# Gates of four chunks computed as one batch on 128 partitions, in an mLSTM and feed-forward kernel

## The chip, the cores and the metric

One core of one Trainium2 chip. The metric is the device time of one launch in microseconds (us), which is the time of that core.

## The reference

Four sequences in a batch of 8 heads, 768 steps, head size 40, go through a recurrent mLSTM layer, and its output through a feed-forward layer:

```python
for t in range(S):
    m_new = np.maximum(f_gate[:, :, t] + m, i_gate[:, :, t])
    f_stab = np.exp(f_gate[:, :, t] + m - m_new); i_stab = np.exp(i_gate[:, :, t] - m_new); m = m_new
    C = f_stab * C + i_stab * v_t k_t^T          # one 40 x 40 state per sequence and head
    n = f_stab * n + i_stab * k_t
    y[:, :, t] = sigmoid(o_gate) * (C q_t) / max(|n q_t|, 1)
h = x @ w_in                                      # 3072 x 320 by 320 x 2048; x is y
g = h where h >= 1, 0 where h <= -1, (h + 1)^2 / 4 between
out = g @ w_out                                   # 2048 x 320
```

The two weights arrive as 8-byte floats and are turned into 4-byte ones on the chip.

## The kernel before

**Chunks and units.** The 768 steps are cut into six chunks of L = 128 steps, c = 0 to 5. Within a chunk the recurrence is written as matrix products. A unit n = 4c + b is chunk c of batch entry b, with its eight heads. For a unit: `score` (q k products on TensorE, 16 records `psa<-raw`), `decay` (eight exponentials on ScalarE into `Abc`), the product with the values (`psa<-v,Abc`, here called PV), the part from the state (`psa<-C,qn`), the normalizer `z`, the factor `sz` and the output `y` on VectorE, three transposes of `y` on TensorE (`psa<-ident,y`), and `xh`, `xl`, the high and low part of the transposed output. `carry_on` (L549) adds the unit to the state `C` (records `psa<-ow` or `psa<-v,vk`); between chunks GpSimd multiplies the state by `dec`.

**Gates.** For each chunk, `gate_sums` (L195), `gate_tail` (L241) and `gate_exps` (L255) work on 32 partitions, one for each pair of batch entry and head, 128 steps along the row. VectorE scans the running maximum `m` from the last chunk's `carry`; sums and differences give the log decays `a`; their coarse part `ah` and their rest are scanned into `ac` and `al`; four rows of 32 are collected in `ex`, transposed by one matmul, and exponentiated into `G`. `ac` is stored to memory (`a_d`) and loaded back spread over 128 partitions as `Abc`; the decay of the state goes through `dx`, `dc_d` and three loads of 4-byte elements into `dec` (`decays`, L293). Chunk 0 is done at the start (on 96 partitions, three copies of the 32). Chunk 1 is the `g1` at the end of STEPS, its tail after the first block of the loop. Chunks 2 to 5 are given out one step at a time from the loop steps 2, 13, 28 and 43 (GATES_AT, L51).

**The front.** STEPS (L57) is a written order of all engines' work up to the four units of chunk 0: `s` scores, `x` decays, `m` score products, `u` PV, `y`, `z`, `t` the rest of a unit, `E`, `A` exponents, `L` loads, `c`, `e`, `d` the conversion of the first weight slice, `wN` N matmuls on zeros ahead of the next ones.

**The loop.** Six token tiles of 512 (j) by 16 slices of 128 hidden columns (fc) make 96 steps x. `mm1` (L683), here block x, is eight matmuls into one of two PSUM buffers `psh`; ScalarE takes a ReLU and a square, VectorE the last step `r`, which frees the buffer. `mm2`, here product x, comes two steps later and adds to four PSUM buffers `pso`: eight records for j = 0, 24 after that. `slot` puts the pieces of the mLSTM units of the next token tile between the blocks.

**The weights.** Sixteen slices, in 0 to in 7 and out 0 to out 7, are loaded (`wraw`, two buffers) and converted by ScalarE (`mg`, and `wh` for the in slices), GpSimd and VectorE (`win`, `ow`, `mg`, `wl`). Block 2i and 2i + 1 need in i, products 2i and 2i + 1 need out i. A slice's load waits until the slice two before it is read.

**What sets the order.** Each engine runs its queue in order. Within STEPS the written order holds; after it, a scheduler places the instructions of each engine. All loads and stores are issued by SyncE (SP) to one queue. Tiles of the `gate` pool lie where those of the pool `mo` (`r`, `gh`, `gl`) come to lie after it is closed:

```python
    front = False
    gates.close()
    mo = ctx.enter_context(tc.tile_pool(name="mo", bufs=2))
```

Of the kernel before, what the change touches and what calls it, by code (L numbers as in the profile page):

```python
# [98 lines left out]
def mlstm_ffn_kernel(ctx, tc, qk, qn, vk, og, fi0, fi, w_in, w_out, cst, out):  # L99
# [95 lines left out]
    def gate_sums(c):  # L195
        pool, i, f = gsrc.pop(c)

        NP = NSEQ if c else 3 * NSEQ
        new = lambda name, p=NP, n=L, bufs=1: pool.tile([p, n], F32, name=name if c else name + "0", bufs=bufs)
        k = 1  # L200
        m, a, ah, ac = new("m", n=L + 1, bufs=k), f, new("ah", bufs=k), new("ac")
        al = ah

        ex = exs[c] = new("ex", P)
# [699 lines left out]
```

## Time and profile before

| | us |
|---|---|
| three timed runs | 519.98, 520.55, 523.67 |
| their median | 520.55 |
| span of the profiled execution, first to last instruction | 521.0 |

The profile is one execution taken by the hardware profiler. It gives no other time of its own than the span. Engines are PE (TensorE matmuls), PEld (its weight loads), DVE (VectorE), ACT (ScalarE), POOL (GpSimd) and SP (SyncE). Busy time is the time in which an instruction of the engine runs. Line numbers in rows of the trace are mostly those of the recording helper (L82 and L85), so that rows are told apart by the names of their tiles.

### The profile page before, as it was taken

How to read it: one execution, taken by the hardware profiler on the slowest of the kernel's cores; microseconds unless marked ns; L12 is line 12 of the kernel's file. 1: busy time of each engine (PE TensorE's matmuls, PEld its weight loads, DVE VectorE, ACT ScalarE, POOL GpSimd, SP SyncE). 2: the span in 40 equal slices, each digit the busy share in tenths (PEclk: the TensorE clock that was granted, in tenths of full speed). 3: DMA queues.
4: the chain of work that ended last, by engine and by line, in shares of the span. 5: the costliest groups of instructions: out<-in, count | busy, mean ns of one | idle time of the engine just before them, and what ended most of it. 6: DMA issues, size and time to landing. Idle time of an engine off the chain costs nothing. (4 is left out here: it accounts for less than half of the span.)

```text
span 521.0 us, 8909 instructions
## 1 busy us (share of the span) xinstructions
PE 493.2 (95%) x3396; PEld 419.9 (81%) x3399; DVE 355.5 (68%) x669; ACT 291.5 (56%) x576; POOL 144.3 (28%) x140
## 2 busy tenths in 40 slices
PE   8984999899898999989999989999999999999996
PEld 4753777678677889968898978889897889988986
DVE  4689987589669697777666778857656755534342
ACT  4626785345187745567643758554477544456553
POOL 2336624243334062242241344413220210000000
PEclk8987999979899999999999999999999999999999
DMA  7848555464441122343121254213432000010001
GB/s 234 274 138 295 155 155 172 110 211 133 131 144 42 26 81 87 89 129 96 45 87 41 82 173 127 72 62 95 146 102 77 15 1 2 0 52 1 1 1 51
DMA packets 29647, 51.30 MB, mean 98 GB/s; under 512 B 10124, under 2 KB 20004, under 8 KB 29604
## 3 DMA queue, kind: packets, MB, share of 16 engines
q1 hardware_dynamic: 29604, 50.72, 31.6%
q8 instruction: 27, 0.44, 0.4%
q14 instruction: 16, 0.13, 0.1%
HBM read 46.67 MB, written 4.04 MB: 97 GB/s over the span
## 5 line engine op out<-in xcount | busy, mean ns | idle before, releaser
L82 ACT ACTIVATE r<-psh,half 128x512 f32<-128x512 f32 x96 | 65.2, 684 | 102.8 <-PE psh L82 100.6
L82 PE MATMUL psh<-xh,wh 128*128 128x512 f32 x288 | 104.5, 419 | 10.1 <-DVE r L82 9.0
L82 DVE SCALAR_TENSOR_TENSOR r<-psh,r 128x512 f32<-128x512 f32 x96 | 65.9, 686 | 70.7 <-ACT r L82 69.8
L82 PE MATMUL pso<-oh,gh 128*128 128x320 f32 x320 | 99.2, 313 | 1.1 <-ACT gh L82 1.1
L82 PE MATMUL psh<-xh,wl 128*128 128x512 f32 x288 | 100.1, 401 | 0.0
L82 PE MATMUL pso<-ow,gh 128*128 128x320 f32 x320 | 98.6, 310 | 0.0
L82 PE MATMUL pso<-oh,gl 128*128 128x320 f32 x320 | 93.4, 313 | 0.2 <-DVE gl L82 0.2
L82 DVE TENSOR_TENSOR gl<-r,gh 128x512 fp32r<-128x512 f32 x80 | 62.3, 779 | 34.1 <-ACT gh L82 33.6
L82 ACT CAST gh<-r 128x512 fp32r<-128x512 f32 x80 | 49.4, 618 | 54.7 <-DVE r L82 52.3
L82 PEld LDWEIGHTS psh<-xh,wh 128*128 128x128 f32 x288 | 51.2, 193 | 20.0 <-DVE r L82 10.9
L82 PEld LDWEIGHTS psh<-xh,wl 128*128 128x128 f32 x288 | 55.0, 192 | 13.3 <-DVE m L85 0.4
L82 PEld LDWEIGHTS pso<-oh,gh 128*128 128x128 f32 x320 | 60.1, 188 | 5.1 <-ACT gh L82 1.7
L82 PEld LDWEIGHTS pso<-ow,gh 128*128 128x128 f32 x320 | 60.1, 188 | 2.8
L82 ACT ACTIVATE r<-r 128x512 f32<-128x512 f32 x96 | 60.4, 631 | 2.4
L82 PE MATMUL psh<-xl,wh 128*128 128x512 f32 x192 | 61.2, 400 | 0.0
L82 PEld LDWEIGHTS pso<-oh,gl 128*128 128x128 f32 x320 | 58.3, 188 | 1.5 <-DVE gl L82 0.8
L82 ACT ACTIVATE Abc<-Abc,nA 128x128 f32<-128x128 f32 x160 | 49.9, 393 | 1.5 <-POOL Abc L82 1.5
L82 POOL TENSOR_TENSOR v<-vk,G 128x328 f32<-128x328 f32 x36 | 32.0, 894 | 60.1 <-issue 33.6
L82 PEld LDWEIGHTS psh<-xl,wh 128*128 128x128 f32 x192 | 36.7, 191 | 8.2
L82 PE MATMUL pso<-ow,r 128*128 128x320 f32 x128 | 39.7, 454 | 1.0 <-DVE ow L82 1.0
L82 POOL TENSOR_SCALAR_AFFINE_SELECT Abc<-Abc 128x1024 f32<-128x1024 f32 x20 | 26.7, 1339 | 44.9 <-DMA Abc<-a_d 29.2
L82 POOL TENSOR_TENSOR C<-C,dec 120x369 f32<-120x369 f32 x16 | 14.0, 875 | 87.4 <-PE psa L82 87.4
(187 smaller groups left out, 719.6 us busy)
## 6 DMA issues: line engine op xcount, KB each, us to landing
Abc<-a_d SPq DMA_DIRECT2D x20, 512.0 KB
raw<-in_qk SPq DMA_DIRECT2D x48, 160.0 KB
vk<-in_vk SPq DMA_DIRECT2D x20, 324.0 KB
wraw<-in_w_in SPq DMA_DIRECT2D x8, 768.0 KB
wraw<-in_w_out SPq DMA_DIRECT2D x8, 640.0 KB
sig<-in_og SPq DMA_DIRECT2D x6, 640.0 KB
out<-r SPq DMA_DIRECT2D x24, 160.0 KB
qn<-in_qn SPq DMA_DIRECT2D x20, 180.0 KB
```

The costliest lines, as they stand in the source:

```text
L82: r = getattr(self.engine, name)(*args, **kwargs)
```

## The change

Chunks 1 to 4 get their gates at once, on 128 partitions (32 for each chunk), in the front and right behind it. Each partition scans its own history: a new input `fic` holds for chunk c the gates of chunks 1 to c, padded ahead with values that leave the running maximum as it is, 512 steps in all; the start is chunk 0's last maximum, which is now computed on all 128 partitions. The five steps are B0 to B4 in STEPS: B0 the scan on VectorE in the middle of the front, B1 and B3 on GpSimd, B2 on VectorE, B4 the four transposes, exponentials and the loads of `dec` for all four chunks. Tiles of the batch lie in the `gate` pool. Chunk 5 keeps the old way, from loop step 34. The diff's other edits rename the pieces of a unit in STEPS (`r`, `f`, `y`, `t`, `z` for `y`, `z`, `t`), split the work on `z`, `sz` and `y` at more places, and give `z` four buffers and `sz` two.

```diff
-GATES_AT = (2, 13, 28, 43)
+GATES_AT = 34
+NB = 4
...
-    "Lg Li Lo Lq0 Lv0 Lq1 Lw0 Lf Lq2 Lv2 Lq3 Lw1 Lc o w9 E0 g0 p A0 k0 x00 w2 s0 x01 m00 w1 E1 A1 h0 v0 x10 m01 w2 s1 "
-    "x11 v1 m10 c w2 u0 m11 w2 E2 A2 x20 w2 s2 y0 x21 v2 m20 m21 w2 u1 z0 w2 E3 A3 x30 e w2 s3 v3 y1 x31 t0 m30 m31 "
-    "w2 u2 z1 y2 w2 u3 t1 z2 y3 w2 t2 z3 t3 d g1 "
+    "Lg Li Lo Lq0 Lv0 Lq1 Lw0 Lq2 Lf Lv2 Lq3 Lw1 Lc o w9 E0 g0 q0 p A0 k0 x00 w2 s0 x01 m00 w1 E1 A1 h0 v0 x10 m01 w2 s1 "
+    "x11 v1 m10 c w2 u0 m11 w2 E2 A2 x20 B0 w2 s2 r0 f0 y0 x21 v2 m20 m21 w2 u1 t0 w2 E3 A3 x30 e w2 s3 v3 r1 f1 y1 x31 z0 "
+    "m30 m31 w2 u2 t1 r2 f2 y2 w2 u3 z1 t2 r3 f3 y3 w2 z2 t3 z3 d B1 B2 B3 B4 "
...
+    def batch_loads():
+        s = batch["s"] = gate.tile([P, 2, NB * L], F32, name="fi_s")
+        nc.sync.dma_start(s, fic)
+    def batch_maxima():
+        s = batch["s"]
+        m = gate.tile([P, NB * L + 1], F32, name="m_s")
+        nc.vector.tensor_copy(m[:, 0:1], batch["first"])
+        nc.vector.tensor_tensor_scan(out=m[:, 1:], data0=s[:, 0, :], data1=s[:, 1, :], initial=m[:, 0:1],
+                                     op0=ALU.add, op1=ALU.max)
+        batch["m"] = m[:, (NB - 1) * L:]
+    def batch_decays():
...
+        nc.gpsimd.tensor_tensor(out=a, in0=f, in1=m[:, :L], op=ALU.add)
+        nc.gpsimd.tensor_tensor(out=a, in0=a, in1=m[:, 1:], op=ALU.subtract)
+        nc.gpsimd.tensor_scalar(out=ah, in0=a, scalar1=CLAMP, scalar2=GRID, op0=ALU.max, op1=ALU.add)
+        nc.gpsimd.tensor_scalar(out=ah, in0=ah, scalar1=-GRID, scalar2=None, op0=ALU.add)
+        nc.gpsimd.tensor_copy(carry, m[(NB - 1) * NSEQ:, L:])
+    def batch_sums():
...
+        nc.vector.tensor_tensor_scan(out=ac, data0=rst, data1=ah, initial=0.0, op0=ALU.mult, op1=ALU.add)
+        nc.sync.dma_start(a_d[1:NB + 1].rearrange("c s l -> (c s) l"), ac)
+        nc.vector.scalar_tensor_tensor(out=a, in0=a, scalar=CLAMP, in1=ah, op0=ALU.max, op1=ALU.subtract)
...
+        nc.vector.tensor_tensor_scan(out=al, data0=rst, data1=a, initial=0.0, op0=ALU.mult, op1=ALU.add)
+    def batch_tail():
...
+        eng = nc.gpsimd
+        eng.tensor_tensor(out=a, in0=i, in1=m[:, 1:], op=ALU.subtract)
+        eng.tensor_tensor(out=a, in0=a, in1=al, op=ALU.subtract)
+        eng.tensor_tensor(out=dh, in0=ac[:, L - 1:].broadcast_to([P, L]), in1=ac, op=ALU.subtract)
+        eng.tensor_tensor(out=dh, in0=dh, in1=a, op=ALU.add)
+        eng.tensor_tensor(out=dh, in0=dh, in1=al[:, L - 1:].broadcast_to([P, L]), op=ALU.add)
...
+        eng.tensor_tensor(out=dcu, in0=ac[:, L - 1:], in1=al[:, L - 1:], op=ALU.add)
+    def batch_exps():
+        tp = psum_a()
+        hot(tp)
+        for k, x in enumerate(batch["q"]):
+            nc.tensor.transpose(tp[:, k * P:(k + 1) * P], x, ident)
...
+        nc.scalar.activation(Gv[:, 0:3], tv[:, 0:3], AF.Exp)
+        nc.scalar.activation(Gv[:, 3], tv[:, 3], AF.Exp, scale=-1.0)
+        nc.scalar.mul(nA[:, 1:NB + 1, :], tv[:, 2], -1.0)
+        dx = gate.tile([P, D], F32, name="dx")
+        nc.scalar.activation(dx, batch["dc"].broadcast_to([P, D]), AF.Exp)
+        nc.sync.dma_start(dc_d[1:NB + 1].rearrange("c b (h d) -> (c b h) d", d=D), dx)
         for g, h0 in enumerate(GROUPS):
-            nc.sync.dma_start(dec[:, g, :, c0], dc_d[c0, :, h0 * D:(h0 + 3) * D].rearrange("b x -> x b"))
+            nc.sync.dma_start(dec[:, g, 1:NB + 1, :],
+                              dc_d[1:NB + 1, :, h0 * D:(h0 + 3) * D].rearrange("c b x -> x c b"))
...
-            if x in GATES_AT:
-                c = 2 + GATES_AT.index(x)
-                load_gates(later, c, c + 1)
-                steps = gate_steps(c)
-            if x >= GATES_AT[0]:
+            if x == GATES_AT:
+                load_gates(later, NB + 1, NB + 2)
+                steps = gate_steps(NB + 1)
+            if x >= GATES_AT:
...
-            if x == 0:
-                with tc.issue_after(mark["r", "dve"].ins):
-                    run(gate_tail(1))
-                    gate_exps(1)
```

The instructions move as follows. TensorE, before, from the last transposes of the front (`psh<-ident,y`) on; blocks 0 and 1 are the rows `psh<-xh,...` and `psh<-xl,...`:

```order
L85 MATMUL psh<-ident,y 128x128 x3
L82 MATMUL psh<-xh,wh 128x512 x4
L82 MATMUL psh<-xh,wl 128x512 x2
L82 MATMUL psh<-xl,wh 128x512 x2
L82 MATMUL psh<-xh,wh 128x512
L82 MATMUL psh<-xh,wl 128x512 x3
L82 MATMUL psh<-xl,wh 128x512 x2
```

And now, at the same place; `psa<-ow` are the state updates of units 0 and 1, `fi_s`, `ac_u` and `ah_u` the batch's tiles:

```order
L86 MATMUL psh<-ident,y 128x128 x3
L83 MATMUL psa<-ow 120x123 x6
L86 MATMUL psh<-ident,fi_s 128x128
L83 MATMUL psh<-xh,wh 128x512 x2
L83 MATMUL psh<-xh,wl 128x512 x2
L83 MATMUL psh<-xl,wh 128x512 x2
L83 MATMUL psh<-xh,wh 128x512
L83 MATMUL psh<-xh,wl 128x512
L86 MATMUL psh<-ident,fi_s 128x128
L86 MATMUL psh<-ident,ac_u 128x128
L86 MATMUL psh<-ident,ah_u 128x128
```

Two state updates and a transpose of the batch stand ahead of block 0, three transposes ahead of block 1; the batch takes one of the two buffers `psh`.

ScalarE, before, from the last cast of the front to the first ReLU and square of the loop (`r<-psh,half`, `r<-r`):

```order
L85 CAST xh<-psh 128x3x128
L82 ACTIVATE mg<-wraw 128x768
L82 CAST wh<-win 128x3x256
L82 ACTIVATE mg<-wraw 128x640
L82 ACTIVATE r<-psh,half 128x512 x2
L82 ACTIVATE r<-r 128x512
```

And now; `mg<-wraw` of 768 columns are in 1, in 2 and in 3, of 640 columns out 0 and out 1:

```order
L86 CAST xh<-psh 128x3x128
L83 ACTIVATE mg<-wraw 128x768
L83 CAST wh<-win 128x3x256
L83 ACTIVATE mg<-wraw 128x640
L83 ACTIVATE mg<-wraw 128x768
L86 ACTIVATE G<-psh 128x3x4x32
L86 ACTIVATE G<-psh 128x4x32
L86 ACTIVATE nA<-psh 128x128
L86 ACTIVATE dx<-dc_u 128x40
L83 CAST wh<-win 128x3x256
L83 ACTIVATE mg<-wraw 128x640
L83 ACTIVATE mg<-wraw 128x768
```

The next row is the ReLU of blocks 0 and 1. Ahead of it stand now the first steps on in 2, out 1 and in 3, and the batch's exponentials.

SyncE's queue, before, from chunk 1's store of its decays on (`wraw<-in_w_in` is in 3, then in 4, `wraw<-in_w_out` out 2, then out 3):

```order
L82 DMA dc_d<-dx 32x40
L82 DMA wraw<-in_w_in 128x1536
L82 DMA ow<-in_vk 128x648
L82 DMA wraw<-in_w_out 128x1280
L82 DMA dec<-dc_d 120x4x1 x3
L82 DMA wraw<-in_w_in 128x1536
L82 DMA wraw<-in_w_out 128x1280
```

And now, from the batch's store of `ac_u` on (the `wraw` rows are in 2, out 1, in 3, out 2, in 4):

```order
L86 DMA a_d<-ac_u 128x128
L83 DMA wraw<-in_w_in 128x1536
L83 DMA Abc<-a_d 128x1024 x3
L83 DMA wraw<-in_w_out 128x1280
L83 DMA wraw<-in_w_in 128x1536
L86 DMA dc_d<-dx 128x40
L83 DMA ow<-in_vk 128x648 x2
L83 DMA wraw<-in_w_out 128x1280
L86 DMA dec<-dc_d 120x16x1 x3
L83 DMA wraw<-in_w_in 128x1536
```

The three loads of `Abc` stand now ahead of out 1 and in 3, and the loads of `dec` move 16 elements a partition where they moved 4.

## Rows read from the trace of the kernel before

**Rows 1.** The page, busy time of each engine, its share of the span and its number of instructions.

```profile
PE 493.2 (95%) x3396; PEld 419.9 (81%) x3399; DVE 355.5 (68%) x669; ACT 291.5 (56%) x576; POOL 144.3 (28%) x140
```

**Rows 2.** The table by stage: stretch and its length in us, then busy time and number of instructions of each engine (PE, PEld, DVE, ACT, POOL), the granted TensorE clock as a share of full speed (the two levels are 1.2 and 2.4 GHz), the busy share of the DMA engines, and GB/s.

```profile
33.60:45.65 12.05, 5.36 (x16) 3.66 (x16) 11.87 (x23) 5.90 (x10) 7.96 (x5) 0.78 0.77 258
45.65:49.20 3.55, 3.55 (x8) 2.81 (x9) 3.55 (x11) 0.41 (x2) 1.38 (x4) 0.50 0.95 314
...
100.00:112.00 12.00, 9.15 (x49) 7.66 (x48) 10.76 (x21) 3.90 (x9) 4.96 (x5) 0.72 0.73 238
130.00:144.00 14.00, 12.14 (x69) 9.16 (x67) 9.93 (x20) 1.46 (x3) 5.09 (x5) 0.88 0.41 122
166.00:420.00 254.00, 249.53 (x1947) 220.29 (x1947) 182.90 (x337) 151.35 (x306) 74.77 (x68) 1.00 0.28 84
```

**Rows 3.** The chain that ended last: a block, eight matmuls that follow each other, at full clock; start and length.

```profile
333.30 1.86 PE psh L82 x8
```

**Rows 4.** The timeline of TensorE at the start of the loop: start, length, instruction, number, and in brackets the idle time before it with what ended it. The first row is the start of block 0, the last one the start of block 2.

```profile
33.60 2.08 PE L82 MATMUL psh<-xh,wh 128*128 128x512 f32 x4 [0.57 <-ACT xh L85]
...
45.65 1.22 PE L82 MATMUL psh<-xh,wh 128*128 128x512 f32 x2 [6.69 <-DVE r L82]
```

**Rows 5.** The timeline of VectorE in the front and at the start of the loop: a scan of 128 elements in the front, a wait for ScalarE, the scan of chunk 1's gates, and the first `r`.

```profile
2.93 0.48 DVE L85 TENSOR_TENSOR_SCAN m<-fi,m 96x128 f32<-96x128 f32 x1 [2.00 <-DMA fi<-in_fi]
...
26.50 0.42 DVE L85 TENSOR_TENSOR xl<-psa,xh 128x256 fp32r<-128x256 f32 x1 [3.10 <-ACT xh L85]
...
36.64 1.23 DVE L85 TENSOR_TENSOR_SCAN m<-fi_t,m 32x128 f32<-32x128 f32 x1
...
44.91 0.69 DVE L82 SCALAR_TENSOR_TENSOR r<-psh,r 128x512 f32<-128x512 f32 x1
```

**Rows 6.** The timeline of SyncE: start and length of the issue of each transfer, or of several.

```profile
37.69 0.33 SPq L82 DMA_DIRECT2D wraw<-in_w_in  x1
...
44.59 1.28 SPq L82 DMA_DIRECT2D Abc<-a_d  x3
...
89.95 1.38 SPq L82 DMA_DIRECT2D dec<-dc_d  x3
...
91.96 1.69 SPq L82 DMA_DIRECT2D Abc<-a_d  x1
...
167.87 1.59 SPq L82 DMA_DIRECT2D dec<-dc_d  x3
```

**Rows 7.** The timeline of GpSimd: its half of the conversion of in 1, the scaling of two units' keys by `G`, and the selects on `Abc`, the last of them for unit 7.

```profile
35.44 2.22 POOL L82 TENSOR_SCALAR win<-wraw 128x768 uint16<-128x768 uint16 x1 [5.09 <-issue]
...
37.74 2.32 POOL L82 TENSOR_TENSOR ow<-ow,G 128x328 f32<-128x328 f32 x2
...
48.81 5.44 POOL L82 TENSOR_SCALAR_AFFINE_SELECT Abc<-Abc 128x1024 f32<-128x1024 f32 x3 [0.64 <-DMA Abc<-a_d]
...
96.79 1.09 POOL L82 TENSOR_SCALAR_AFFINE_SELECT Abc<-Abc 128x1024 f32<-128x1024 f32 x1 [4.43 <-DMA Abc<-a_d]
```

**Rows 8.** The timeline of ScalarE: the first step on in 2, a ReLU of the loop, the eight decays of unit 7, and the square that stands behind the decays.

```profile
44.91 0.92 ACT L82 ACTIVATE mg<-wraw 128x768 f32<-128x768 f32 x1 [1.26 <-DVE ow L82]
...
53.94 0.69 ACT L82 ACTIVATE r<-psh,half 128x512 f32<-128x512 f32 x1 [1.69 <-PE psh L82]
...
97.92 2.45 ACT L82 ACTIVATE Abc<-Abc,nA 128x128 f32<-128x128 f32 x8 [1.50 <-POOL Abc L82]
100.27 0.61 ACT L82 ACTIVATE r<-r 128x512 f32<-128x512 f32 x1
```

**Rows 9.** The timeline of TensorE in the loop's first 16 steps: the state updates of units 0 to 2, a score and a PV at full clock, then rows of the stretches 100 to 112 and 130 to 144, with the products of one step (`pso<-ow,r`, 16 records) as they are at full clock at 126.18.

```profile
56.01 0.80 PE L82 MATMUL psa<-ow 128*120 128x123 f32 x6
...
61.13 1.43 PE L82 MATMUL psa<-ow 128*120 128x123 f32 x12
...
66.03 1.16 PE L82 MATMUL psa<-raw 40*128 40x128 f32 x16
...
89.63 1.92 PE L82 MATMUL psa<-v,Abc 128*128 128x41 f32 x16
...
102.11 0.90 PE L82 MATMUL psa<-C,qn 120*128 120x123 f32 x6 [1.92 <-DVE C L82]
...
103.49 2.37 PE L82 MATMUL psa<-v,Abc 128*128 128x41 f32 x16 [0.48 <-DVE xh L82]
...
106.71 2.41 PE L82 MATMUL psa<-raw 40*128 40x128 f32 x16 [0.46 <-ACT nA L82]
109.06 2.07 PE L82 MATMUL psh<-xh,wh 128*128 128x512 f32 x4
...
126.18 4.47 PE L82 MATMUL pso<-ow,r 128*128 128x320 f32 x16
...
132.39 1.95 PE L82 MATMUL psa<-v,Abc 128*128 128x41 f32 x16 [0.79 <-DVE xh L82]
...
135.95 6.06 PE L82 MATMUL pso<-ow,r 128*128 128x320 f32 x16 [0.49 <-DVE ow L82]
```

**Rows 10.** The DMA view of three stretches, 50 to 56, 169 to 170 and 170 to 171 us: packets and megabytes moved in each, and how many packets were small.

```profile
DMA packets 1578, 1.94 MB, mean 324 GB/s; under 512 B 1155, under 2 KB 1155, under 8 KB 1578
...
DMA packets 836, 0.00 MB, mean 4 GB/s; under 512 B 835, under 2 KB 836, under 8 KB 836
...
DMA packets 652, 0.00 MB, mean 3 GB/s; under 512 B 652, under 2 KB 652, under 8 KB 652
```

More of the change, by code (lines that the diff above doesn't have):

```diff
@@ L98, in mlstm_ffn_kernel @@
 @with_exitstack
-def mlstm_ffn_kernel(ctx, tc, qk, qn, vk, og, fi0, fi, w_in, w_out, cst, out):
+def mlstm_ffn_kernel(ctx, tc, qk, qn, vk, og, fi0, fi, fic, w_in, w_out, cst, out):
     nc = Core(tc)
@@ L146, in mlstm_ffn_kernel @@
     dc_d = dr.tile([NC, B, H * D], F32, name="dc_d")
-    dec = const.tile([120, 3, B, NC], F32, name="dec")
+    dec = const.tile([120, 3, NC, B], F32, name="dec")
     carry = const.tile([NSEQ, 1], F32, name="carry")
-    nc.vector.memset(carry, -1e30)
     def parts3(x, name, eng):
@@ L180, in mlstm_ffn_kernel @@
     gsrc = {}
+    batch = {}
     exs = {}
@@ L196, in gate_sums @@
         pool, i, f = gsrc.pop(c)
[L198 to L204, printed above, removed]
+        new = lambda name, p, n=L: pool.tile([p, n], F32, name=name if c else name + "0", bufs=1)
+        m = new("m", NSEQ if c else P, L + 1)
         if c:
@@ L209, in gate_sums @@
         nc.vector.tensor_tensor_scan(out=m[:, 1:], data0=f, data1=i, initial=m[:, 0:1], op0=ALU.add, op1=ALU.max)
+        if c == 0:
+            batch["first"] = m[:, L:]
         yield
-        nc.vector.tensor_tensor(out=a, in0=f, in1=m[:, :L], op=ALU.add)
+        NP = NSEQ if c else 3 * NSEQ
+        m, i, a, ah, ac = m[:NP], i[:NP], f[:NP], new("ah", NP), new("ac", NP)
+        al = ah
+        ex = exs[c] = new("ex", P)
+        nc.vector.tensor_tensor(out=a, in0=a, in1=m[:, :L], op=ALU.add)
         nc.vector.tensor_tensor(out=a, in0=a, in1=m[:, 1:], op=ALU.subtract)
@@ new lines, in batch_decays @@
+    def batch_decays():
+        f, m = batch["s"][:, 0, (NB - 1) * L:], batch["m"]
+        a = batch["a"] = f
+        ah = batch["ah"] = gate.tile([P, L], F32, name="ah_u")
+        nc.gpsimd.tensor_tensor(out=a, in0=f, in1=m[:, :L], op=ALU.add)
[3 more added lines that the diff above has]
+        nc.gpsimd.tensor_copy(carry, m[(NB - 1) * NSEQ:, L:])
@@ new lines, in batch_tail @@
+    def batch_tail():
+        i, m, ac, al = batch["s"][:, 1, (NB - 1) * L:], batch["m"], batch["ac"], batch["al"]
+        a, dh = i, batch["a"]
+        eng = nc.gpsimd
[4 more added lines that the diff above has]
+        eng.tensor_tensor(out=dh, in0=dh, in1=al[:, L - 1:].broadcast_to([P, L]), op=ALU.add)
+        dcu = batch["dc"] = gate.tile([P, 1], F32, name="dc_u")
+        eng.tensor_tensor(out=dcu, in0=ac[:, L - 1:], in1=al[:, L - 1:], op=ALU.add)
+        batch["q"] = a, dh, ac, al
@@ L561, in carry_on @@
             C = state[b]
-            nc.gpsimd.tensor_tensor(out=C, in0=C, in1=dec[:, :, b, c:c + 1].broadcast_to([120, 3, 3 * D1]),
+            nc.gpsimd.tensor_tensor(out=C, in0=C, in1=dec[:, :, c, b:b + 1].broadcast_to([120, 3, 3 * D1]),
                                     op=ALU.mult)
@@ L746, in mlstm_ffn_kernel @@
         elif what == "Lf":
-            load_gates(mid, 1, 2)
+            batch_loads()
+        elif what[0] == "B":
+            (batch_maxima, batch_decays, batch_sums, batch_tail, batch_exps)[n]()
         elif what == "Lc":
@@ L764, in mlstm_ffn_kernel @@
         elif what[0] == "g":
-            run(gate_sums(n))
+            sums = gate_sums(n)
+            for _ in range(4):
+                next(sums)
+        elif what[0] == "q":
+            run(sums)
         elif what[0] == "k":
@@ L790, in mlstm_ffn_kernel @@
             heat = int(what[1:])
-        elif what[0] in "uytz":
+        elif what[0] in "urfytz":
             if what[0] == "u":
@@ L874, in _layout @@
     a["fi"] = np.stack([f_gate.reshape(NSEQ, S), i_gate.reshape(NSEQ, S)], axis=1)
-    a["fi0"] = np.concatenate([a["fi"][:, :, :L]] * 3)
+    a["fic"] = np.zeros((NB, NSEQ, 2, NB * L), np.float32)
+    a["fic"][:, :, 1] = -1e30
+    for c in range(NB):
+        a["fic"][c, :, :, (NB - 1 - c) * L:] = a["fi"][:, :, L:(c + 2) * L]
+    a["fic"] = a["fic"].reshape(P, 2, NB * L)
+    a["fi0"] = np.concatenate([a["fi"][:, :, :L]] * 4)
     w = moe_w_in.view(np.int64)
```

33 lines of the change are left out of this document (17 added, 16 removed).

## The prediction

> **What bounds the kernel now.** Read first the page: TensorE is busy for 493.2 of the 521.0 us [rows 1], so 27.8 us of idle time are all that better order could win, with what a low clock costs beside them. Read next the table by stage, to see where that idle time lies. From 166 to 420 us it is 4.5 of 254 us, at full clock [rows 2]: VectorE is busy there too, but TensorE hardly waits for it. Taking the gates of chunks 4 and 5 off VectorE in that stretch removes nothing that ends a wait; I give it 0.5. The low clock and the large waits stand in three places:
>
> - The loop's start, 33.60 to 45.65: TensorE works for 5.36 of 12.05 us, and after it the granted clock is 0.50, 1.2 of 2.4 GHz [rows 2]; a block that takes 1.86 us at full clock [rows 3] takes 3.55 there. Block 2 waits 6.69 us for the first `r`, which frees its buffer [rows 4]. VectorE is busy for 11.87 of the 12.05 us [rows 2], chunk 1's gates (the 1.23 us scan is one of their rows) among the work ahead of that `r`, which runs at 44.91 [rows 5].
> - Stall A, 100 to 112: 9.15 us busy of 12, clock 0.72 [rows 2]. Unit 7's `Abc` is issued at 91.96 [rows 6], its select starts 4.83 us later [rows 7], the eight decays (2.45 us) follow on ScalarE, and behind them in its queue the square of a block, at 100.27 [rows 8]. VectorE's `r`, and the state sum behind it, come after. Three waits of TensorE, 1.92, 0.48 and 0.46, make 2.86. The low clock makes the score 2.41 instead of 1.16, PV 2.37 instead of 1.92, and four matmuls 2.07 instead of 0.93, half of the block above [rows 3, 9]: 2.84 more, and 12 x 0.28 = 3.4 by the clock. I take 3.2; stall A costs 6.1.
> - Stall B, 130 to 144: waits of 0.79 and 0.49, and products that take 6.06 instead of 4.47 [rows 9]: 2.9, which the clock of 0.88 [rows 2] bears out (14 x 0.12 = 1.7).
>
> **The change part by part.** *Front.* The padded scan is 512 elements long on VectorE, and no row shows such a one. Bounds: a 128-long scan takes 0.48 [rows 5], so between 0.48 and 4 x 0.48 = 1.9; I take 1.6, nearer the upper end, as each element waits for the one before it. It stands before unit 0's step on `r`, and VectorE has 3.10 us of idle time at 26.50 [rows 5] that take the delay up. The new input is 128 x 1024 x 4 bytes, 0.52 MB: at most 1.6 us more of the queue at 324 GB/s [rows 10]. Cost 0; 1.6 if that cover is gone.
>
> *Loop start.* VectorE loses chunk 1's gates, so it is no longer what block 2 waits for; what is late next is the release of ScalarE. In the new order the first ReLU stands behind the `mg` of in 3 (before, only behind that of out 0), and VectorE's first `r` behind in 3's three steps. So in 3 must have landed. Its load stands behind in 2 (issued 37.69 as before, since in 1's conversion on GpSimd still ends at 35.44 + 2.22), three `Abc` and out 1: 0.79 + 1.57 + 0.66 + 0.79 = 3.80 MB of queue, 11.7 us at 324 GB/s [rows 6, 7, 10]. From 38.8 on (1.1 us after the issue) that ends at 50.5; the last bytes show some 1.4 us later, as a first `Abc` issued at 44.59 was taken up 4.22 us later [rows 6, 7], of which 1.6 are its bytes. in 3 is there at 51.9; `mg` 0.92, two ReLUs 0.69 each [rows 8] and a square of 0.61 make 54.8, `r` 0.69 [rows 5] makes 55.5. Block 2 starts at 55.6 where it started at 45.65: +10.0. Bounds: 52.5, if the bytes pass faster or `r` comes with the first ReLU alone, to 59, if GpSimd's conversion of in 3 takes 2.2 us again and stands behind a select of 1.8 [rows 7].
>
> The batch's steps on GpSimd lie under this. The scalings of units 0 and 1 end at 40.06 as before [rows 7]; five steps of 128 elements, each at most 0.45 by those scalings of 328 elements in 1.16, end at 42.3; the transposes, block 1 at half clock and the exponentials end before 50. Chunk 1's store of `dx` and the wait of `r` for it (they share memory) end there too. GpSimd's nine steps therefore cost nothing, but at 4 us more they would still be hidden.
>
> *Work moved into the wait.* TensorE does the state updates of units 0 to 2 before block 2, 0.80 + 1.43 us [rows 9]: -2.2. Two transposes of `ex` go, -0.3; the conversions that are ahead when block 2 starts (in 2, in 3, out 1) save the small waits for `ow`: -0.5.
>
> *The loads of `dec`.* Before, three loads of 120 x 4 elements of 4 bytes, 1,440 packets; those issued at 167.87 [rows 6] are the 836 and 652 packets of 169 to 171 us, at next to no GB/s [rows 10]: some 1.9 us of all queues. Now all four chunks come at once, 5,760 packets, so 7.5 us. They stand ahead of in 4 in SyncE's order, so that in 4 lands near 66.3 instead of 60, and VectorE's conversion of in 4 stands in its order before the `r` for which block 4 waits. Block 4 then waits 1.8 and block 6 another 1.2: +3.0. Bounds: 0, if small packets and large pass side by side, to 7, if all the time shows. I take 3.0 because the load of `Abc` issued at 91.96, 2.0 us behind the loads of `dec` at 89.95 [rows 6], took 4.83 us to its select, 0.6 more than the first `Abc`'s 4.22, though no weights are in front of it.
>
> The Trainium skill, "DMA: Bandwidth & Descriptors", section "Queues, rings and completion order", says that "On each SDMA engine descriptors are consumed in ring order". This speaks against the change: by it in 4 waits out the small packets. The 0.6 us just named agree, for a quarter of the packets. By this rule the term is +3.0, without it 0.
>
> *Stalls.* All of `G`, `nA` and the decays of units 4 to 19 are there early. In the new order PV of unit 4 is followed by blocks 8 to 11 before the next unit's steps, so that a late select has over 7 us of cover: stall A goes, -6.1. Stall B goes as it stood, -2.9, but near PV of unit 6 and block 14 the pieces crowd: a wait for `xh` of 0.5 and one for in 7's conversion of 1.3, as VectorE and GpSimd take in 7 behind more of the units' work, and 1.6 of half clock after them as in stall B: +3.4.
>
> Sum, on the profiled execution: 10.0 - 2.2 - 0.3 - 0.5 + 3.0 - 6.1 - 2.9 + 3.4 - 0.5 = +3.9, so 521.0 becomes 524.9. The median of the timed runs, 520.55, is 0.45 below that span; against it I forecast 524.4, rounded to 524.
>
> **The rivals.** *Faster, 516.* The waits that I add are not there: the small loads pass beside in 4 (-3.0), and no new stall stands near unit 6 (-3.4), since three slices are converted when block 2 starts; block 2 starts 2 us earlier. 524.4 - 3.0 - 3.4 - 2.0 = 516. For it: TensorE in the loop is 249.53 of 254 busy once it has a lead [rows 2]. Against it: the first 16 steps are those in which all engines convert.
>
> *Slower, 530.* Stall A comes again at unit 7: its `Abc` is still a load that starts when PV frees the buffer, and its eight decays still stand ahead of a square in ScalarE's order. The price is the 6.1 worked out above: 530.5. It decides when the select ends later than the 7 us of cover, that is if the load, with raw and weights before it, takes over 6 us instead of 4.83. For it: the same 4.83 was too late before. Against it: the order now puts four blocks (4 x 1.86) there.
>
> *No net change, 520.* The restart comes at 52.5, the lower bound, and the other terms hold (521.3), or the change only fills the wait with other work and the loads of `dec` cost nothing as well (518.3). For it: TensorE idles 6.69 us there already; against it: the written order holds the first ReLU behind in 3.
>
> **How the numbers follow.** The forecast has 0.50, the faster rival 0.18, the slower one 0.20, no net change 0.12. One per cent of 520.55 is 5.2 us, about what a measurement of this kernel can tell from no change: the limits are 515.3 and 525.8. The forecast's own range, by its bounds at the restart (-3 to +3.5) and at `dec`, is 519 to 528; some two fifths of it lie above 525.8. Slower: 0.20 + 0.36 x 0.50 = 0.38. Faster: most of the first rival, as its time lies at the limit and the gains can be larger (stalls A and B both gone without a successor), 0.16. Within 1%: 0.46. The range that leaves 2 in 10 out is 515 to 531.
>
> **What would show it right or wrong.** Block 0 should start at 33.6, within 0.2, or the scan was not hidden. Block 2 should start at 55.6, behind a first ReLU that follows in 3's `mg` at once; a ReLU near 42 or a start below 50 breaks the largest term. Blocks 4 and 6 should wait for `r`, that `r` behind VectorE's step on in 4, and in 4's load should be issued right behind `dec` and land some 10 us later; if it lands in 4, the term of 3.0 is nothing. The stretch of units 4 to 7 should have no wait over 1 us except near PV of unit 6 and block 14. The prediction is wrong if the stretch from 166 us on changes by over 1 us, if GpSimd ends a wait of TensorE, or if stall A's waits come again while unit 7's decays run.

## The result and the profile after

Five runs of each kernel, median 525.51 us after (524.80 to 526.04) and 522.13 before (519.98 to 523.67): ratio 1.0074, 95% interval 1.0048 to 1.0099 (the two medians alone lie 0.65% apart). The change made the kernel slower by 0.74%, which 520.55 turns into 524.4; the forecast was 524. The profiled execution of the kernel after has a span of 523.7 us and took 525.51, so that 1.8 us lie around a span; the one before has 521.0, which with the same 1.8 makes 522.8, above the median. I had set that span against the median of runs; from span to span the change is +2.7. A span is that of one execution, and executions differ: the last transposes of the front of the kernel before start at 32.48 us in the one profiled here and at 30.21 in the one of e7, whose front is the same. A difference of two spans by 2 us is therefore no finding by itself; differences within one stretch, and medians with their intervals, say more.

The page after, busy time of each engine (before: [rows 1]):

```profile
PE 493.0 (94%) x3396; PEld 420.7 (80%) x3399; DVE 341.9 (65%) x607; ACT 289.2 (55%) x559; POOL 140.8 (27%) x147
```

TensorE does the same work (493.0 us) in a longer span; VectorE has 13.6 us less to do, and the span is no shorter for it. The table by stage, columns as in [rows 2]:

```profile
33.60:45.65 12.05, 6.19 (x24) 5.08 (x24) 10.30 (x15) 2.62 (x4) 8.60 (x10) 0.64 0.74 256
45.65:49.20 3.55, 2.97 (x7) 2.39 (x8) 2.32 (x3) 1.48 (x5) 2.35 (x2) 0.50 0.97 357
49.20:56.00 6.80, 1.26 (x4) 0.54 (x4) 5.54 (x5) 3.19 (x5) 6.56 (x7) 0.50 0.74 243
...
100.00:112.00 12.00, 12.00 (x67) 9.85 (x66) 8.38 (x15) 5.13 (x8) 3.38 (x4) 1.00 0.45 139
112.00:130.00 18.00, 16.01 (x88) 12.46 (x87) 12.50 (x24) 7.79 (x16) 6.67 (x8) 0.90 0.43 140
130.00:144.00 14.00, 14.00 (x69) 11.20 (x68) 10.56 (x22) 4.42 (x7) 4.27 (x5) 0.88 0.24 80
...
166.00:420.00 254.00, 251.41 (x1962) 222.96 (x1963) 181.26 (x322) 151.53 (x300) 75.23 (x69) 1.00 0.26 83
```

The idle time at the loop's start now reaches to 56 us; the stretch of stall A, 100 to 112, is full and at full clock; a new stall stands in 112 to 130. The start of each block in the two traces shows where time is lost and given back (a block's place among the units' pieces differs between kernels, so that single differences swing by what was moved past it):

| block | before | after | difference |
|---|---|---|---|
| 0 | 33.60 | 39.40 | +5.80 |
| 2 | 45.65 | 57.97 | +12.32 |
| 11 | 92.83 | 105.13 | +12.30 |
| 12 | 109.06 | 111.61 | +2.55 |
| 16 | 144.96 | 150.26 | +5.30 |
| 20 | 162.62 | 168.69 | +6.06 |
| 48 | 304.06 | 305.52 | +1.47 |
| 94 | 505.73 | 508.02 | +2.29 |

The timeline of TensorE after, up to block 2, which [rows 4] answer to (columns as there):

```profile
36.34 2.82 PE L83 MATMUL psa<-ow 128*120 128x123 f32 x12 [4.60 <-POOL ow L83]
...
39.40 1.20 PE L83 MATMUL psh<-xh,wh 128*128 128x512 f32 x2
...
46.23 1.22 PE L83 MATMUL psh<-xh,wh 128*128 128x512 f32 x2 [3.59 <-ACT nA L86]
...
55.55 1.58 PE L83 MATMUL psa<-ow 128*120 128x123 f32 x6 [5.54 <-POOL ow L83]
...
57.97 1.22 PE L83 MATMUL psh<-xh,wh 128*128 128x512 f32 x2
```

Three waits, 13.7 us together, where one of 6.69 stood: the state updates ahead of block 0 wait for GpSimd's scaling, block 1 for the batch's exponentials, which hold one of the two buffers `psh`, and the third update for GpSimd again. At 57.97 no wait is shown, but only because the update and two records of a score ahead of it filled it: the first `r` ends at 57.92. The chain that ended last, in the same stretch (start, length, what):

```profile
39.27 8.73 DMA Abc<-a_d
...
48.05 2.21 POOL v L83 x2
50.27 1.28 POOL Abc L83
...
51.68 1.03 POOL ow L83
...
52.73 0.83 DVE ow L83
53.56 1.38 DVE win L83
54.94 0.99 DVE mg L83
...
56.02 0.09 DVE win L83
...
57.24 0.69 DVE r L83
57.97 3.78 PE psh L83 x8
```

Read it from below: block 2 waits for `r`, `r` for VectorE's three steps on in 3, these for out 1's last step, that for GpSimd's half of out 1, and that stood behind two scalings and a select in GpSimd's queue, which had waited for the batch's `Abc`. How much each had to do with it, the rows of VectorE and ScalarE tell, with what each had waited for:

```profile
49.58 1.07 DVE L83 TENSOR_SCALAR ow<-wraw 128x640 uint16<-128x640 uint16 x1 [0.61 <-DMA wraw<-in_w_out]
...
52.73 0.83 DVE L83 SCALAR_TENSOR_TENSOR ow<-mg,ow 128x640 int32<-128x640 int32 x1 [0.79 <-POOL ow L83]
```

```profile
53.59 0.90 ACT L83 ACTIVATE mg<-wraw 128x768 f32<-128x768 f32 x1 [3.23 <-DVE ow L83]
...
55.54 0.63 ACT L83 ACTIVATE r<-r 128x512 f32<-128x512 f32 x1
```

out 1 landed only at 49.57; GpSimd's half of it came 0.79 us after VectorE was ready for it. ScalarE's first step on in 3 (53.59) waited for VectorE's last step on out 1, not for in 3's bytes, and ScalarE's square for the first `r` ended at 56.17, 1.1 us before VectorE came to that `r`.

### The profile page after: what moved, and what is told of

Same layout as the page of the kernel before. It is cut to its first block, busy times and chain, and to the rows that moved or that the text cites. A ratio compares the mean times of both kernels' runs of the same rounds, so it can differ in the third digit from the quotient of the medians.

```text
span 523.7 us, 8797 instructions
## 1 busy us (share of the span) xinstructions
PE 493.0 (94%) x3396; PEld 420.7 (80%) x3399; DVE 341.9 (65%) x607; ACT 289.2 (55%) x559; POOL 140.8 (27%) x147
## 4 chain that ended last, share of the span: by engine, by line
PE 81%; DVE 7%; ACT 6%; DMA 4%; issue 1%; POOL 1%; ACTq 0%; SPq 0%; DVEq 0%; POOLq 0%
PE psh L83 33%; PE pso L83 33%; PE psa L83 15%; DMA Abc<-a_d 2%; ACT Abc L83 1%; ACT L83 1%; DMA ow<-in_vk 1%; ACT r L83 1%; DVE win L83 1%; ACT Abc L86 1%; DMA out<-r 1%; ACT sig L83 0%; DVE win L86 0%; DVE r L83 0%; POOL v L83 0%
## 5 line engine op out<-in xcount | busy, mean ns | idle before, releaser
L83 PE MATMUL pso<-oh,gh 128*128 128x320 f32 x320 | 100.3, 316 | 2.4 <-ACT gh L83 2.2
L83 PE MATMUL psh<-xh,wl 128*128 128x512 f32 x288 | 101.2, 405 | 0.0
L83 PE MATMUL psh<-xl,wh 128*128 128x512 f32 x192 | 62.4, 405 | 0.0
L83 POOL TENSOR_TENSOR v<-vk,G 128x328 f32<-128x328 f32 x36 | 30.4, 850 | 69.0 <-issue 46.8
L83 POOL TENSOR_SCALAR_AFFINE_SELECT Abc<-Abc 128x1024 f32<-128x1024 f32 x20 | 25.1, 1254 | 50.6 <-DMA Abc<-a_d 40.0
L83 PE MATMUL pso<-ow,r 128*128 128x320 f32 x128 | 38.0, 437 | 0.0
L83 POOL TENSOR_TENSOR m<-m 128x1024 bf16<-128x1024 f32 x12 | 24.2, 2013 | 47.0 <-DVE m L83 47.0
```

The source lines that it names most:

```text
L83: r = getattr(self.engine, name)(*args, **kwargs)
```

## The experiments

All are compared with runs of the kernel before on the same chip; the spans are those of one profiled execution each.

**e1. The batch in a pool of its own.** `ah_u`, `ac_u`, `dc_u` and `dx` are moved like `fi_s`. `r` shares no memory with the batch, and the scheduler puts the first ReLU behind in 2's first step instead of in 3's.

```diff
+    bt = ctx.enter_context(tc.tile_pool(name="bt", bufs=1))
...
-        s = batch["s"] = gate.tile([P, 2, NB * L], F32, name="fi_s")
+        s = batch["s"] = bt.tile([P, 2, NB * L], F32, name="fi_s")
...
```

> The batch's tiles lie in a pool of their own, so that r no longer shares memory with them; the scheduler then puts the first ReLU behind in 2's first step and the first r ahead of the steps on out 1 and in 3. Theory A (block 2 starts late because r stands behind the conversion of in 3, and that delay is what the change loses): block 2 starts at 48 to 50 instead of 57.97 us, and 5 to 7 us of it last to the end: span 517 to 519, faster than the kernel before by about half a per cent. Rival B (the weights' arrival and conversion bound the first steps in any order): block 2 starts early, but blocks 4 to 8 wait for the slices instead, the lead is gone by block 11, and the span stays at 523.7 within 1.5.

Median 521.69, ratio to before 1.0009 (0.9987 to 1.0032), span 520.4. Block 2 starts at 49.83, block 11 9.1 us earlier than in the kernel after; at block 94 4.2 are left, and of the span 3.3. Theory A holds for the start, and for less than half of what it wins; its span of 517 to 519 was not reached. The rest goes between blocks 11 and 16; the timeline of TensorE there:

```profile
101.67 0.90 PE L83 MATMUL psa<-C,qn 120*128 120x123 f32 x6 [0.31 <-DVE C L83]
103.05 1.95 PE L83 MATMUL psa<-v,Abc 128*128 128x41 f32 x16 [0.48 <-DVE xh L83]
...
107.20 2.07 PE L83 MATMUL psa<-raw 40*128 40x128 f32 x14 [1.78 <-DVE hv L83]
109.20 2.07 PE L83 MATMUL psh<-xh,wh 128*128 128x512 f32 x4
```

State, PV and score of neighbouring units follow each other with no block between; each needs one of two buffers `psa` back from VectorE, and the clock falls: from 107 to 111.5 us 0.50 is granted, and the last four matmuls take 2.07 as in stall A [rows 9].

**e2. Conversions behind `r`.** The argument of `split_next` names the mark behind which ScalarE's and VectorE's steps of a conversion are issued.

```diff
-                    split_next()
+                    split_next("r" if x else "x")
```

> The conversions of in 2 and of all later slices are issued behind the last block's r; the batch stays in the shared pool, so that the first r still waits for the store of dx. Theory A: block 2 starts at 50 to 52 us (dx at 47, its store some 2 us, ReLU, square and r), span 518 to 520. Rival B: what block 2 gains is lost at blocks 4 to 6, for which the slices now come late: span 523 or more.

Median 526.75, ratio 1.0112 (1.0084 to 1.0140), span 523.6. Block 2 at 52.47, near the 52 of theory A, and blocks 4 to 6 did not wait as B has it: from 56 to 130 us TensorE is busy all the time and block 14 stands 14.3 us ahead of the kernel after. From block 14 to 16 all but 0.9 of it is lost:

```profile
56.00:100.00 44.00, 44.00 (x222) 33.29 (x221) 38.05 (x55) 32.19 (x55) 15.27 (x15) 1.00 0.59 204
100.00:130.00 30.00, 30.00 (x150) 23.14 (x151) 20.30 (x35) 13.16 (x27) 6.58 (x7) 1.00 0.29 87
130.00:166.00 36.00, 29.24 (x199) 25.25 (x197) 21.09 (x43) 16.51 (x37) 14.15 (x15) 0.76 0.47 145
```

(The table by stage, columns as above.) The units' pieces were put off; block 16 needs the output of units 4 to 7, so that they stand together ahead of it: 6.8 us idle and a clock of 0.76. The span that B names came true, for a reason B did not name.

**e3. `dec` late.** Each chunk's loads behind the first `Abc` of the chunk; the order on the other engines is the same.

```diff
+        load_dec(1)
+
+    def load_dec(c):
         for g, h0 in enumerate(GROUPS):
-            nc.sync.dma_start(dec[:, g, 1:NB + 1, :],
-                              dc_d[1:NB + 1, :, h0 * D:(h0 + 3) * D].rearrange("c b x -> x c b"))
+            nc.sync.dma_start(dec[:, g, c, :], dc_d[c, :, h0 * D:(h0 + 3) * D].rearrange("b x -> x b"))
...
+            if x in (12, 24, 40):
+                c = {12: 2, 24: 3, 40: 4}[x]
+                with tc.issue_after(mark[4 * c, "A"].ins):
+                    load_dec(c)
```

> Of dec only chunk 1 is loaded ahead of in 4, chunks 2 to 4 each behind the load of Abc of their first unit; the order on all other engines is the same, instruction by instruction. By the prediction's term (blocks 4 and 6 wait for in 4 behind the small packets): 3.0 us shorter, span 520.7. Rival (what the trace after suggests: in 4 comes some 3 us earlier, but no block waits for it, since r stood behind other work): same span within 1 us, 523.7, with in 4 taken up near 59.5 instead of 62.7.

Median 525.62, ratio 1.0090 (1.0063 to 1.0117), span 523.6; block 16 0.11 us earlier, block 94 0.13. The term of 3.0 is nothing, though in 4 did come earlier. SyncE and VectorE after, then in e3:

```profile
53.15 4.43 SPq L86 DMA_DIRECT2D dec<-dc_d  x3
57.75 0.98 SPq L83 DMA_DIRECT2D wraw<-in_w_in  x1
...
62.69 0.62 DVE L83 TENSOR_SCALAR win<-wraw 128x768 uint16<-128x768 uint16 x1 [1.55 <-DMA wraw<-in_w_in]
```

```profile
53.27 1.43 SPq L86 DMA_DIRECT2D dec<-dc_d  x3
55.19 0.36 SPq L83 DMA_DIRECT2D wraw<-in_w_in  x1
...
61.16 1.47 DVE L83 TENSOR_SCALAR win<-wraw 128x768 uint16<-128x768 uint16 x1
```

With the wide loads SyncE issues in 4 2.6 us later, and VectorE waits 1.55 for it; in e3 it waits for nothing. TensorE waits in neither.

**e4. The nine steps on VectorE** (`nc.gpsimd` to `nc.vector` in B1 and B3, two small ones with them: the copy of `carry` and `dc_u`).

> All nine gate steps of the batch on VectorE instead of GpSimd. By the prediction (GpSimd's steps lie under the wait for in 3 and cost nothing, nor would VectorE's): block 2 starts at 57 to 59.5 and the span stays within 2 us of 523.7. Rival (GpSimd's queue, in which the conversions of out 1 and in 3 stand behind the selects, sets the start of block 2): with nine steps less on GpSimd the state updates start at 34 instead of 36.3, block 2 at 55 to 56, span 521 to 522.

Median 534.96, ratio 1.0261 (1.0232 to 1.0290), span 532.8. Both theories fall: 9 us slower than the kernel after. ScalarE's ReLU and VectorE's first `r`:

```profile
56.80 1.26 ACT L83 ACTIVATE r<-psh,half 128x512 f32<-128x512 f32 x2 [0.85 <-DMA dc_d<-dx]
```

```profile
62.61 0.60 DVE L83 TENSOR_SCALAR win<-wraw 128x768 uint16<-128x768 uint16 x1 [1.32 <-DMA wraw<-in_w_in]
63.10 0.68 DVE L83 SCALAR_TENSOR_TENSOR r<-psh,r 128x512 f32<-128x512 f32 x1
```

The steps delay the store of `ac_u` (issued 40.18 instead of 34.37) and the exponentials (50.10 instead of 45.37). ReLU then waits for the store of `dx`, whose memory `r` takes, and the scheduler puts the first `r` behind the first step on in 4, one slice further: block 2 starts at 63.83, 5.9 us later than in the kernel after; most of the other 3.4 are lost between blocks 12 and 16. In this order GpSimd is the better engine for these steps; at the loop's start it is the place of `r` that is expensive.

**e5, e6. Another buffer for the batch's transposes**, on top of e1; e6 adds e2's edit.

```diff
     def batch_exps():
-        tp = psum_a()
+        tp = ps_a.tile([P, 512], F32, name="psa")
```

> As the first experiment (the batch's tiles in a pool of their own), and the batch's transposes go to a buffer psa instead of one of the two psh. In the scheduled order blocks 0 and 1 now stand ahead of the state updates of units 0 and 1, and the first ReLU directly behind out 0's first step. Theory A (a block started earlier is worth its time): block 2 starts at 44 to 46 us instead of 49.83 in the first experiment, and at least 3 of these 5 us are left at the end: span 515 to 517.5. Rival B (what is won before block 11 is given back where the units' pieces crowd, between 95 and 150 us): the end moves by 1 us or less: span 519.5 to 521.

> As e5, and the conversions of in 2 and of later slices issued behind the last block's r. Theory A: block 2 at 43 to 45 us, span 514 to 517. Rival B: the slices come later, blocks 4 to 6 wait, and the time is given back at the latest where the units' pieces crowd: span 519.5 to 522.

e5: median 518.13, ratio 0.9940 (0.9919 to 0.9961), span 517.5; block 2 at 46.52. e6: 518.49, 0.9957 (0.9940 to 0.9974), span 516.6; block 2 at 44.19. Both beat the kernel before. The waits of 4.60, 3.59 and 5.54 are gone, and in e5 1.25, 1.00, 0.38 and 2.03 us stand for them up to block 2. e5 lies at the upper end of A, and of e6's lead of 13.7 us on the kernel before at block 12 1.2 are left at block 18. Between them A and B both hold: the early start counts, and what is ahead of need is lost where the pieces crowd.

**e7. The kernel before, `dec` of chunk 2 behind `Abc` of unit 8** (as in e3, at step 12, for c = 2 alone); same order elsewhere.

> The kernel before, with the three loads of dec of chunk 2 behind the load of Abc of unit 8; the order on all other engines is the same. By the prediction's chain for stall A (late Abc of unit 7, its decays ahead of the square, r, the state sum): the select of unit 7 starts 1.0 us earlier (the load takes 3.8 us as in the kernel after, instead of 4.83), the wait of 1.92 us shrinks by as much, and the span by 1 to 1.5 us, to about 519.7. Rival (the crowding of the units' pieces sets that stretch): the waits move to the next pieces and the span stays within 0.5 us of 521.0.

Median 520.48, ratio 0.9980 (0.9959 to 1.0001). This profiled execution has block 0 at 31.32 instead of 33.60, so that its span of 516.7 can't be compared; the stretch can. GpSimd's select, then TensorE's waits:

```profile
92.74 1.09 POOL L82 TENSOR_SCALAR_AFFINE_SELECT Abc<-Abc 128x1024 f32<-128x1024 f32 x1 [3.11 <-DMA Abc<-a_d]
```

```profile
98.06 0.90 PE L82 MATMUL psa<-C,qn 120*128 120x123 f32 x6 [0.59 <-DVE C L82]
99.44 2.38 PE L82 MATMUL psa<-v,Abc 128*128 128x41 f32 x16 [0.48 <-DVE xh L82]
...
102.66 2.42 PE L82 MATMUL psa<-raw 40*128 40x128 f32 x16 [0.46 <-ACT nA L82]
```

`Abc`, issued at 88.85, reaches the select in 3.89 instead of 4.83 us, and 1.92 becomes 0.59; from block 11 to 12 it is 14.91 instead of 16.23 us. So the chain that I read there is real and worth 1.3 us; the timed runs, 1.0 with an interval of about as much on both sides, don't prove it by themselves. Its own issue took 1.69 us behind the loads of `dec` [rows 6], and here:

```profile
88.85 0.35 SPq L82 DMA_DIRECT2D Abc<-a_d  x1
```

The other 4.8 of stall A's 6.1 are still there: waits of 0.59, 0.48 and 0.46, and the score and PV at half clock (2.42 and 2.38). No run here takes these away by themselves, so what causes them stays open.

**e8. The kernel after with an extra small load** ahead of the scores' inputs.

> The kernel after, with an extra load of chunk 1's gates (32 x 2 x 128 elements, whose result nothing reads) at the place where the kernel before has it, ahead of the scores' loads. Theory (that load held up raw of the first units, so that its removal made the front 1.6 us shorter): the last front transposes start at 32.2 to 32.5 us again instead of 30.87, and the state updates, which wait for GpSimd, move by less than 0.5 us if GpSimd's chain does not hang on the front, or by 1.3 to 1.6 if it does; span 523.7 to 525.2. Rival (the pieces of the units written in another order made the front shorter): the front stays as it is.

Median 526.38, ratio 1.0106 (1.0075 to 1.0136), span 523.7. The front ends 1.33 us later (32.20), the state updates start 1.47 later (37.81), block 2 at 58.11: the wait at the loop's start takes the front's delay up. Whether this load made the front shorter stays open, since the front of the kernel before itself ended at 32.48 in one execution and at 30.21 in e7's.

**e9, e11, e12. The units spread.** Steps of units 4 to 7: 0, 3, 6, 9 on top of e5 (e9) and on the kernel after (e11); 3, 6, 8, 10 on the kernel before (e12), which can't have unit 4 sooner.

```diff
-OFFS = [3, 5, 7, 9, 14, ...
+OFFS = [0, 3, 6, 9, 14, ...
```

> As e5, with units 4 to 7 placed three steps apart, from two or three steps earlier (the steps of their pieces 0, 3, 6, 9 instead of 3, 5, 7, 9), which the batch allows since their gates are there. Theory C (the waits between 95 and 135 us come from the units' pieces following each other through two buffers psa, one waiting for the other's vector work, so that what was won before them is given back): the waits of 0.31, 0.48, 1.43 and 0.79 us and the half clock behind them go by half or more, span 513.5 to 516 instead of 517.5. Rival D (the total of the vector and scalar work in this stretch bounds it, wherever the pieces stand): span 517 to 518.5, with the waits at other pieces.

> The kernel after with nothing changed but the steps of units 4 to 7 (0, 3, 6, 9 instead of 3, 5, 7, 9); block 2 still stands behind in 3's conversion. If e9's gain over e5 (4.5 us) comes from the crowding alone, it comes here too: block 2 at 57 to 59, no wait over 1 us between 112 and 150, span 518.5 to 520.5. If it needs the early start (e5's pool and buffer), since the late start already gave the units' inputs time, span 522 to 524.

> The kernel before with the steps of units 4 to 7 at 3, 6, 8, 10 instead of 3, 5, 7, 9; without the batch unit 4 can't stand before step 3, as chunk 1's gates end in step 0. Theory C (crowding costs what stalls A and B show, 6.1 and 2.9 us, and any spreading takes some of it): 517 to 519.5 us on the median, against some 521.5 for the kernel before. Rival (only the room ahead of step 3 that the batch opens helps; moved back, the pieces crowd against block 16, which needs unit 7): 521 to 524.

e9: median 513.29, ratio 0.9842 (0.9813 to 0.9871), span 513.0. e11: 522.58, 1.0032 (1.0009 to 1.0056), span 520.6. e12: 525.15, 1.0070 (1.0045 to 1.0096), span 522.5. The table by stage in e9:

```profile
100.00:112.00 12.00, 9.90 (x57) 8.49 (x56) 10.53 (x17) 4.87 (x9) 2.27 (x2) 0.78 0.56 170
112.00:130.00 18.00, 18.00 (x89) 14.55 (x89) 15.39 (x30) 9.61 (x17) 7.50 (x8) 0.95 0.39 136
130.00:144.00 14.00, 13.95 (x104) 10.01 (x103) 6.11 (x11) 4.65 (x13) 4.73 (x4) 1.00 0.33 100
```

Stall B is gone, and e9 is 4.5 us of span, 1.0% by the ratios, faster than e5: theory C, with a span half a us below its range. The gain lies behind block 12 (to block 16 it takes 32.68 us, in e5 37.73); in the first stretch a wait of 2.10 and a low clock are left, so that C's halving does not hold there. The spread alone brings the kernel after 3.1 us of span, 0.4% by the ratios (e11; block 2 is late there as ever, at 56.67), just outside the first branch of its expectation, and no wait over 1 us stands between 112 and 150. On the kernel before the spread that its gates allow makes it slower (e12), against theory C and beyond the rival's 521 to 524: from block 12 to 16 it takes 38.85 us there instead of 35.90, as the pieces crowd ahead of block 16 instead. So e9, the fastest of all and faster than both kernels, rests on the batch, which lets unit 4 stand at step 0; other spreads on the kernel before were not tried.

**e10. The gate steps of a chunk done over twice on VectorE**, from steps 13 and 24 on, on tiles that nothing reads; `idle_gates` holds the VectorE steps of `gate_sums` and `gate_tail`.

```diff
+            if x in (13, 24):
+                load_gates(later, 3, 4)
+                steps = idle_gates(3)
+            if 13 <= x < GATES_AT:
+                with tc.issue_after(mark["r", "dve"].ins):
+                    next(steps, None)
```

> The kernel after, with the gate steps of one chunk done over on VectorE twice, from loop steps 13 and 24 on, one step at a time as the kernel before has them, on tiles whose results nothing reads; no transposes, exponentials, stores or loads of dec. By the prediction's term (the gates of chunks 4 and 5 are hidden but for 0.5 us): span 523.7 to 524.3, and block 48 less than 0.5 us later. Rival (the kernel after gained 3 us between block 20 and block 48 on the kernel before because VectorE no longer had these steps): 2 to 3 us of it come back, span 525.5 to 526.7.

Median 524.48, ratio 1.0063 (1.0039 to 1.0086), span 522.2: not slower than the kernel after at all. VectorE's busy time is 350.9 us, so that 9.0 of the 13.6 us are back. The stretch from 166 to 420 us:

```profile
166.00:420.00 254.00, 252.19 (x1961) 222.37 (x1960) 185.28 (x336) 151.23 (x301) 75.61 (x69) 1.00 0.26 84
```

VectorE works 4.0 us more there than in the kernel after and TensorE waits 0.8 less. The work as such was hidden, as predicted; block 48 comes 0.2 us earlier, and the span is below the expected range.

## Why the prediction held, and where it did not

*The loop start* (+10.0, block 2 at 55.6). The order was read rightly: the first ReLU and the first `r` stand behind in 3, and taking them from there moves block 2 to 49.83 (e1). The size was 12.3, and the sum that gave 10.0 was built on the wrong waits. It let in 3's landing at 51.9 start ScalarE; ScalarE started at 53.59, when VectorE had ended out 1, and 0.79 of these 1.7 us are GpSimd's half of out 1, behind two scalings and a select (the upper bound had named such a conversion, of in 3). And it let `r` follow ScalarE's square, though it names VectorE's three steps on in 3 ahead of it: these held `r` another 1.1 us. So VectorE, which the prediction had taken off this wait, ended it again. The 9 us of e1 at block 11, of which 3 to 4 reach the end, show what the order costs, e5 what the buffer does.

*GpSimd's steps cost nothing.* True as long as `r` is late: they end at 41.6. In e5, where it is not, TensorE waits 1.25 and 1.00 us for them. That they were estimated at 0.45 at most and took 0.40 to 1.02 did not matter. The expectation of e4, that VectorE could as well have had them, was wrong by 9 us.

*The loads of `dec`* (+3.0). This step failed: the term is nothing (e3). The small packets of the loads passed faster than the 744 a us that I took from [rows 10]; from 57 to 60 us 3,899 of them, about 1,300 a us:

```profile
DMA packets 3916, 0.12 MB, mean 40 GB/s; under 512 B 3899, under 2 KB 3899, under 8 KB 3916
```

in 4 was there at 62.7, not 66.3. And nobody waited for what stood behind it: VectorE's `r` for block 4 ended at 65.43, and block 4 came, without a wait, at 69.21, because block 2 itself came so late. Most of in 4's delay was SyncE's own issue, 4.43 us instead of 1.43, a queue that the prediction had not counted. The same queue is enough for the 0.6 us that it took as a sign for its term, as `Abc` behind the loads of `dec` took 1.69 us to issue and 0.35 in e7. Whether in 4 also waited for what stood ahead of it among the packets, as the Trainium skill has it ("DMA: Bandwidth & Descriptors", section "Queues, rings and completion order"), no run here tells from the late issue: VectorE takes it up 4.9 us after its issue, and 6.0 us after it in e3, there without a wait.

*Stall A* (-6.1). It went, by the order of blocks that the prediction read; but only 1.3 of it was the late `Abc` (e7). The chain was real, and the prediction took the first chain that fitted for the whole price. Which part of the change took the other 4.8 away was not separated.

*Stall B and the new one* (+0.5 together). The new one came at block 14, the place named, with waits of 0.31 and 0.54 before it (for the state and `Abc`, not for `xh`) and this one for in 7's conversion, of the 1.3 predicted:

```profile
129.21 2.07 PE L83 MATMUL psh<-xh,wh 128*128 128x512 f32 x4 [1.14 <-ACT wh L83]
```

Idle time and half clock from 112 to 144 are worth more than before, not the same: 1.99 us idle and clocks of 0.90 and 0.88, against 1.86 idle and clocks of 1.00 and 0.88: about 1.9 us. From 144 to 166 another 1.1 us of idle came (3.34 against 2.19); the longest wait there is one of 1.64, for `gl`, that ends at 166.24.

*The later gates* (-0.5, and two transposes). The stretch from 166 us on has 1.9 us less idle time (2.59 against 4.47 [rows 2]), where "over 1 us" was the mark of an error. e10 shows that it was not VectorE's work: with most of that work back, the idle time is smaller still (1.81). The longest waits there, 1.65 after against 1.26 and 0.88 before, fall on other pieces with every order; what decides them was not settled.

*The signs that were named.* Block 0 started at 39.40, not at 33.6, and not for the scan: the last transposes of the front start at 30.87, earlier than before. The state updates of units 0 and 1 stand ahead of block 0 in the new order and wait for GpSimd's scaling. The prediction has these scalings end at 40.06 and block 0 start at 33.6 all the same, and both can't be; it cost nothing more because block 2 was later still. GpSimd ended two waits of TensorE (4.60 and 5.54), another sign of an error. Blocks 4 and 6 did not wait for `r`. The range of 519 to 528 is narrower than the bounds at the restart and at `dec` make it when they are added, 518 to 532.

By the timed ratio the forecast was good to 0.1%; by the spans +2.7 stands against +3.9. Against that sum +2.3 (loop start), +1.4 and +1.1 (crowding) stand against -3.0 (`dec`) and -1.4 (later, -1.9 where -0.5 was forecast); the -1.6 that are left lie in stall A, the moved work and the last 100 us, which the blocks' times don't tell apart. The sign rested on the largest term, which the experiments confirm; the closeness is luck. The rival on the slower side had the right kind of loss, pieces of units 5 to 7 crowding, not the cause that it named. The diff's other edits (the new order of a unit's pieces in the front, the finer split of `z`, `sz` and `y`, their buffers) were not run without the batch, so that what they add is not shown.

## What to carry to other kernels

Before taking a batch of work as hidden, look at what memory and buffers it borrows: a shared pool moved the first `r` behind a whole weight slice, one of two PSUM buffers was held against block 1, and undoing both turned a loss of 0.7% into a gain of 0.6%. Time won ahead of a stretch in which an engine's pieces crowd is given back there, so that the crowding has to be spread first or at the same time; here that took it to 1.6%. A chain that ends a stall gives its price only when it is shortened by itself: here that gave 1.3 of the 6.1 us.

## What the runs showed of the hardware

Issuing the three loads of `dec` took SyncE 4.43 us for 120 x 16 elements and 1.43 for 120 x 4, with the same number of instructions. Of the three (shortest, middle and longest in ns), in the kernel after and then in e3:

```profile
L86 SPq DMA_DIRECT2D dec<-dc_d x3: 387/1052/2908, 53.2 to 56.5; - x3
```

```profile
L86 SPq DMA_DIRECT2D dec<-dc_d x3: 390/478/479, 53.3 to 54.2; - x3
```

The shortest is the first, issued as fast with 16 elements as with 4; the second and third are held, and so is the load of in 4 behind them (0.98 us, in e3 0.36), which has no small elements. The same three wide loads took 2.78 us in e2 and 5.99 in e9. So the elements of a load don't give the time of its issue; what is queued ahead of it seems to, which no run tests by itself.

Steps of one kind and size on GpSimd took 0.40 and 0.46 us where they read `ac_u` or `fi_s` alone, 1.02 and 0.99 where `ah_u` was the second input, in e1 as in the kernel after:

```profile
21.75 0.53 POOL L86 TENSOR_TENSOR fi_s<-fi_s,m_s 128x128 f32<-128x128 f32 x1
...
38.20 1.02 POOL L86 TENSOR_TENSOR fi_s<-fi_s,ah_u 128x128 f32<-128x128 f32 x1 [0.90 <-DVE ah_u L86]
39.18 0.40 POOL L86 TENSOR_TENSOR fi_s<-ac_u 128x128 f32<-128x128 f32 x1
```

A second input is not the reason by itself: the first row has two and took 0.53, and 0.41 in e2. The two slow steps begin while VectorE is in a step whose two inputs both lie outside PSUM (`win<-mg,win` from 37.97 to 38.90, `wl<-win,wh` from 39.80 to 40.93), the two fast ones do not; but it is so in every run, and none moves these steps apart.

The scan of 512 elements took 1.28 us, against 0.48 for 128 in the front [rows 5] and the 1.6 estimated; a scan of 128 took 1.23 in the same rows, so that the length alone does not set it.
